# Two Fourier and gated layers on one core: the matrix tests in one list, and a later or earlier place for four groups of work

## The chip, the core and the metric

The kernel runs on one core of a Trainium2 chip. The core has a matrix engine (TensorE, PE in the profile, with its weight loads as PEld), VectorE (DVE), ScalarE (ACT), GpSimd (POOL), and SyncE (SP), which here issues the DMAs. Each engine runs its own instructions in order, and waits for the others at semaphores. The metric is the device time of one execution in microseconds; a kernel's time is the median of several runs.

## The reference

x has 2048 rows of 640. Two layers follow each other, each of a Fourier part A and a gated part B, both behind a layer norm and added to x:

```
def _A_ref(x, dft_seq_re, dft_seq_im, dft_hid_re, dft_hid_im):
    a = jnp.einsum("bsd,ed->bse", x, dft_hid_re)
    b = jnp.einsum("bsd,ed->bse", x, dft_hid_im)
    return jnp.einsum("ts,bse->bte", dft_seq_re, a) - jnp.einsum("ts,bse->bte", dft_seq_im, b)

def _B_ref(x, w_gate, w_up, w_down):
    g = jnp.einsum("bsd,df->bsf", x, w_gate)
    u = jnp.einsum("bsd,df->bsf", x, w_up)
    return jnp.einsum("bsf,fd->bsd", _sigmoid(g) * u, w_down)

x = x + _A_ref(_layernorm(x, axis=-1), ...)
x = x + _B_ref(_layernorm(x, axis=-1), ...)
x = x + _A_ref(_layernorm(x, axis=-1), ...)
x = x + _B_ref(_layernorm(x, axis=-1), ...)
```

w_gate and w_up are 640 x 1728, w_down (W2) is 1728 x 640. The Fourier matrices are 2048 x 2048 (sequence) and 640 x 640 (hidden, W_hid here), each with a real and an imaginary part. All are inputs.

## The kernel before, in words

The kernel has a fast version, `folded`, that holds if the Fourier matrices have the symmetries of such matrices and the weights lie in a range, and a slow one, `general`. The fast version runs always, tests its inputs on the way, and writes a flag; the slow one runs behind it if the flag says so, which it does not here. The 100 matrix tests are these: 64 row tests of the sequence matrices (`load_rows`, `test_rows`: 32 for each part, four DMAs of 128 KB each; five VectorE operations, then a square with a sum on ScalarE, `square_rest`), 20 column tests (`load_cols`, `test_cols`), and 10 row tests and 6 column tests of W_hid (`load_hidden_rows`, two DMAs of 160 KB, and `load_hidden_cols`). A test loads into one of three slots (`within(n % 3, ...)`): two stand beside the big memory, the third, "room", is taken from it. In the kernel before, layer 1 tests the real part of the sequence matrix (42 tests), and layer 2 the imaginary part and then W_hid (58 tests, W_hid's last).

Products are made of pairs of float16 parts, a high and a low one, so every operand is split: ScalarE writes the high part, VectorE the rest (`split`, L240 and L242).

A layer goes so. First comes the Fourier part ("he" to "b0" in the marks; layer 1's is in the hand-ordered opening). Then the gated part in two passes over halves of the rows, h = 0 and 1. A pass makes gate and up for tiles of 128 of the 1728 columns: in `seven(j)` and `four(j)` for most (a scheme with fewer products, in which sums of weights and of inputs are multiplied; L1108), in `gate_up` for the first tiles of the first pass (L1064). The results go from PSUM by copies on ScalarE (`snap`, L1112) and additions on VectorE (L1158, L1173); the sigmoid (L1115) and the multiplication `up` (L1188) follow some steps later, by `due(n, ...)`, which counts steps. Then a "down" multiplies by W2: layer 1's first with plain products (`down`, L1250), the other three with the seven combinations of W2's quarters (`stage`, L1364, with `rest_products`, L1345), each of which ends in a VectorE addition to x (`rows_add`, L1238).

The seven combinations of W2 are made once, in layer 1's second pass: `load_forms` (L1274 to L1277, three DMAs of W2 from HBM), `make_forms` (four GpSimd subtractions and a maximum on VectorE, L233), `split_forms` and `keep_forms` (stored to HBM as kept_f); `load_stage(s)` (L1312) loads one combination for a down. In the same way `load_s` (L1037 to L1043) loads the gate weights G, the sums S and the weights U of a tile, planned 15 us ahead of it.

The rows of the second pass are prepared during the first down: `pair_apply` (the norm on ScalarE, L442), `pair_combine` (GpSimd, L492 to L495), `pair_parts` (L507 on ScalarE, L508 on VectorE) and `pair_transpose` (a transposing DMA from the buffer "pb" into XW, L524), for four pairs of row tiles i. Before that, the Fourier results of row groups ("quads") q = 1, 2, 3 are added to x (`combine`, `join_hidden`, `add_hidden`), and statistics made (`pair_stats`, `quad_scale`).

The order is written out by plan: `steps` is the list of TensorE's work, each with a duration written into the code (0.2158 us for a product of 512 columns, for example), T their running sum. `when(t, f, ...)` puts a job before the step that is running at plan time t; jobs of one step are put out in the order of t, and each engine receives its own instructions in that order. start_of(layer, ...) is the plan time of a mark: "c" for `gate_up` steps, "j" for tiles, "d" for a down, "t" for the last narrow tile, "e" for the end of the layer; c0, s0, s1, d0, d1 are short names for such times. The tests are spread over weighted spans of the plan: at_test(n) is the time of the n-th, test n is loaded at at_test(n), tested at at_test(n + 2), squared at at_test(n + 2.6).

All buffers lie in one memory of 390 units of 512 bytes per partition. `take(n, key)` takes the next place from the written list PLACES, and `drop` gives it back; a place that is taken again too early in time is safe, but the writer waits for its last reader.

## Time and profile before

| | us |
|---|---|
| median of 3 runs | 1173.96 |
| lowest, highest | 1173.51, 1175.69 |
| the profiled execution, its own time | 1174.1 |
| its span, first to last instruction | 1172.3 |
| PE, PEld, DVE, ACT, POOL busy | 1101.6, 622.1, 839.7, 577.3, 206.9 |

Stretches of the trace that the text names, from its start: opening 0 to 110; layer 1's `gate_up` 110 to 168, first pass to 256, first down to 350, second pass to 531, second down to 611; layer 2's Fourier part to 655, `gate_up` to 734, first pass to 823, first down to 916, second pass to 1086, second down to the end. In the profile's rows, L12 is line 12 of the kernel before; a group shows "out<-in" by the program's names, its count, its busy time and the mean duration of one in ns, and, behind the bar, the engine's idle time just before such instructions and what ended it. In a view in order of time the first two numbers are start and length, and a number in brackets is the idle time before, with what ended it. SPq is SP's queue of DMA issues.

### The profile page before, as it was taken

What the parts mean: (1) busy time and instruction counts of PE and PEld (TensorE: products, weight loads), DVE (VectorE), ACT (ScalarE), POOL (GpSimd) and SP (SyncE); (2) the same over time, 40 slices, a digit from 0 to 9 for tenths busy, and PEclk for the clock granted to TensorE, in tenths of its full rate; (3) what the DMA queues carried; (4) which work ended last, traced back from release to release, by engine and by line L of the source; (5) the groups of instructions that cost most, each with busy time, mean ns of one, the idle gap of its engine ahead of it and who ended that gap; (6) DMA issues with size and microseconds to landing.
All of it is one profiled execution on the core that took longest, in us unless ns stands there. A gap on an engine that the chain in (4) does not pass through costs nothing.

```text
span 1172.3 us, 17676 instructions
## 1 busy us (share of the span) xinstructions
PE 1101.6 (94%) x6330; PEld 622.1 (53%) x6330; DVE 839.7 (72%) x1642; ACT 577.3 (49%) x1117; POOL 206.9 (18%) x295
## 2 busy tenths in 40 slices
PE   5699999999989898989999999999996999997997
PEld 2467444456764333436777744444674544443675
DVE  7997789758457898788786659966956466632862
ACT  6865547755325555555214544764534345432430
POOL 2210141515322141113020100020412000000211
PEclk9999999999999899999999999999998999999999
DMA  9421874344886777886512038666556765324621
GB/s 267 143 89 58 199 224 169 122 134 162 201 215 233 240 223 254 258 270 194 149 66 80 2 71 185 214 202 191 166 117 153 238 222 172 109 97 133 204 76 71
DMA packets 181912, 192.59 MB, mean 164 GB/s; under 512 B 76314, under 2 KB 145331, under 8 KB 181814
## 3 DMA queue, kind: packets, MB, share of 16 engines
q1 hardware_dynamic: 181174, 188.75, 53.9%
q0 software_dynamic: 640, 2.62, 0.6%
q8 instruction: 51, 0.84, 0.3%
q14 instruction: 47, 0.39, 0.1%
HBM read 143.17 MB, written 31.90 MB: 149 GB/s over the span
## 4 chain that ended last, share of the span: by engine, by line
PE 67%; DMA 15%; DVE 11%; ACT 3%; issue 2%; SPq 1%; POOL 1%; DVEq 0%; ACTq 0%
PE acc L1108 26%; PE acc L1364 14%; PE acc L1064 11%; PE acc L1250 6%; PE acc L858 4%; DMA big<-in_wh 4%; DMA big<-in_ct 3%; PE acc L1345 2%; DMA big<-big 2%; PE acc L776 2%; DVE big L242 1%; PE acc L1217 1%; DMA big<-kept_U 1%; DVE big L1325 1%; DMA big<-kept_f 1%
## 5 line engine op out<-in xcount | busy, mean ns | idle before, releaser
L1108 PE MATMUL acc<-big 128*128 128x512 f16 x2160 | 477.5, 383 | 25.1 <-ACT big L1112 15.6
L1108 PEld LDWEIGHTS <-big 128*128 128x128 f16 x2160 | 212.8, 99 | 288.3 <-issue 33.0
L1364 PE MATMUL acc<-big 128*128 128x320 f16 x1512 | 216.5, 301 | 7.9 <-DVE big L1238 4.7
L1364 PEld LDWEIGHTS <-big 128*128 128x128 f16 x1512 | 148.9, 99 | 68.8 <-issue 7.6
L1112 ACT ACTIVATE big<-acc 128x512 f32<-128x512 f32 x160 | 93.5, 590 | 147.5 <-PE acc L1108 147.2
L1064 PE MATMUL acc<-big 128*128 128x512 f16 (+1 forms) x900 | 156.7, 336 | 0.0
L1415 ACT ACTIVATE big<-big 128x768 f32<-128x768 f32 (+8 forms) x106 | 79.3, 748 | 139.2 <-DVE big L1448 37.5
L1064 PEld LDWEIGHTS <-big 128*128 128x128 f16 x900 | 87.8, 98 | 67.9 <-issue 0.6
L1325 DVE TENSOR_TENSOR big<-big 128x512 f16<-128x512 f32 x126 | 93.9, 760 | 19.1 <-ACT big L1324 18.9
L1250 PE MATMUL acc<-big 128*128 128x320 f16 x656 | 89.6, 299 | 1.2 <-DVE big L242 0.8
L242 DVE SCALAR_TENSOR_TENSOR big<-big 128x640 f16<-128x640 f32 (+7 forms) x94 | 77.7, 850 | 12.6 <-ACT big L240 12.6
L1238 DVE SCALAR_TENSOR_TENSOR big<-acc,big 128x320 f32<-128x320 f32 x112 | 52.8, 484 | 45.5 <-PE acc L1345 24.2
L1324 ACT ACTIVATE big<-big 128x512 f16<-128x512 f32 x126 | 72.0, 616 | 14.8 <-DVE big L1325 7.9
L1250 PEld LDWEIGHTS <-big 128*128 128x128 f16 x656 | 64.2, 98 | 26.6 <-POOL big L1019 1.0
L240 ACT ACTIVATE big<-big 128x640 f16<-128x640 f32 (+8 forms) x94 | 63.5, 705 | 28.2 <-DMA big<-in_wd 11.3
L1339 POOL TENSOR_TENSOR big<-big 128x512 f32<-128x512 f32 x18 | 28.4, 1602 | 250.5 <-DVE big L1325 249.4
L507 ACT ACTIVATE big<-big 128x384 f16<-128x384 f32 (+2 forms) x56 | 36.6, 667 | 51.5 <-DVE big L492 12.4
L508 DVE TENSOR_TENSOR big<-big 128x384 f16<-128x384 f32 (+2 forms) x56 | 45.7, 825 | 20.2 <-ACT big L507 13.3
L1158 DVE TENSOR_TENSOR big<-big,acc 128x512 f32<-128x512 f32 x40 | 27.3, 682 | 41.9 <-PE acc L1108 36.0
L1115 ACT ACTIVATE big<-big 128x512 f32<-128x512 f32 x80 | 49.8, 623 | 13.0 <-DVE big L1158 7.0
L430 POOL TENSOR_SCALAR rowt<-rowt 128x1 f32<-128x1 f32 x24 | 14.6, 609 | 229.5 <-ACT big L429 227.8
L858 PE MATMUL acc<-big 128*128 128x321 f16 (+3 forms) x324 | 49.0, 300 | 2.6 <-DVE big L900 1.5
(193 smaller groups left out, 1264.0 us busy)
## 6 DMA issues: line engine op xcount, KB each, us to landing
big<-in_ct SPq DMA_DIRECT2D x256, 128.0 KB
big<-kept_f SPq DMA_DIRECT2D x63, 320.0 KB
big<-kept_S SPq DMA_DIRECT2D x33, 512.0 KB
big<-kept_w SPq DMA_DIRECT2D x33, 320.0 KB
big<-in_ct SPq DMA_DIRECT2D x32, 256.0 KB
big<-kept_G SPq DMA_DIRECT2D x21, 320.0 KB
kept_S<-big SPq DMA_DIRECT2D x13, 512.0 KB
big<-in_wg SPq DMA_DIRECT2D x19, 320.0 KB
```

Source lines behind the costliest of these rows:

```text
L240: nc.scalar.activation(dh, src, AF.Copy, scale=s)
L242: nc.vector.scalar_tensor_tensor(dl, src, s, dh, op0=OP.mult, op1=OP.subtract)
L858: nc.tensor.matmul(ps[:m, :EC], z[:, at : at + m], w[:, 384 * wp : 384 * wp + EC], start=(d == 0 and zp == HI and wp == HI), stop=(d == ND ...
L1064: nc.tensor.matmul(ps, w[wp][:, d * P : (d + 1) * P], xt[:, xp, :], start=(d == 0 and wp == HI and xp == HI), stop=(d == ND - 1 and wp == LO))
L1108: nc.tensor.matmul(ps, wt, xt, start=start and n == 0, stop=n == len(todo) - 1, skip_group_check=not start)
L1112: nc.scalar.activation(dst, ps, AF.Copy)
L1238: nc.vector.scalar_tensor_tensor(xe, ps[:, :EH], CB, xe, op0=OP.mult, op1=OP.add)
L1250: nc.tensor.matmul(held["pd", i, e][0][:, :EH], held["t", half, j].parts[hp][:, i * P : (i + 1) * P], held["w", 2, j].parts[wp][:, e * EH ...
L1324: nc.scalar.activation(h, v, AF.Copy)
L1325: nc.vector.tensor_tensor(l, v, h, op=OP.subtract)
L1364: nc.tensor.matmul(ps[:, :EH], a[n][hp][:, i * P : (i + 1) * P], w[n][:, wp], start=fresh and m == 0, stop=m == len(todo) - 1, skip_group_ ...
L1415: nc.scalar.activation(v, v, AF.Square, accum_out=new_sum()[:p])
```

## The change

Five things are changed; the steps of TensorE stay the same.

- The tests of both parts stand in one list over both layers, r = 0 first, with W_hid's 16 put in as every fourth test from the 30th on; the spans and their weights are new (layer 1's is weighted 0.5 from its first down to its end), so that 31 tests lie in layer 1 and 69 in layer 2. Slot 2 is taken once for all. The two edge tests stand behind tests 20 and 28. Squares are put at at_test(n + 2.85), not 2.6. In `test_rows`, two VectorE operations of 256 elements become one of 512.
- W2's combinations: the first is loaded 12 us before the second pass (it was 6 us behind its start), one each 21.5 us; make_forms stands 13 us behind its load (it was 5). In the downs, the weights of stage 1 are loaded at d + 0.5 (was d - 7) and of stage 2 at d + 5 (was d + 2).
- Sigmoids are due a step later (3, not 2), and `up` too (5, not 4).
- In layer 2, quads 2 and 3 and their statistics move to the times that layer 1 has, up to some 30 us later; the four pairs of the first down begin at d0 + 8, 22, 49, 62 (were 11, 26, 41, 56), in layer 1 at d0 + 2, 22, 54, 70 (were 2, 22, 42, 62).
- PLACES is a new list.

```diff
-            due(2, lambda: sigmoid(hv(0)))
+            due(3, lambda: sigmoid(hv(0)))
...
-            due(2, lambda: sigmoid(hv(1)))
-            due(4, up)
+            due(3, lambda: sigmoid(hv(1)))
+            due(5, up)
...
     def room():
-        if which[0] == 2:
-            return held["room"].f32
+        if which[0] >= 2:
+            return held["room", which[0]].f32
...
-        nc.vector.tensor_tensor(b, a, b, op=same)
-        nc.vector.tensor_tensor(d, c, d, op=same)
+        bd = v.rearrange("p (g two c) -> p g two c", g=2, two=2)
+        nc.vector.tensor_tensor(bd[:, :, 1], bd[:, :, 0], bd[:, :, 1], op=same)
...
-        for q, u, pace in ((1, q1, 1.2), (2, s0 + 2, 3) if first else (2, c0 + 22, 1.5), (3, s0 + 28, 3) if first else (3, s0 + 6, 2.5)):
+        for q, u, pace in ((1, q1, 1.2), (2, s0 + 2, 3), (3, s0 + 28, 3)):
...
-                when(s0 + ((24, 50) if first else (6, 26))[q] + 4 * i, pair_stats, 1, i, q, True)
-            when(s0 + (70 if first else 46) + q, quad_scale, 2 + q)
+                when(s0 + (24, 50)[q] + 4 * i, pair_stats, 1, i, q, True)
+            when(s0 + 70 + q, quad_scale, 2 + q)
         for i in range(TB):
-            u = d0 + 2 + 20 * i if first else d0 + 11 + 15 * i
+            u = d0 + ((2, 22, 54, 70) if first else (8, 22, 49, 62))[i]
...
-                u = s1 + 6 + 22 * n
+                u = s1 - 12 + 21.5 * n
                 when(u, load_forms, n)
-                when(u + 5, make_forms, n)
+                when(u + 13, make_forms, n)
                 for k in range(2):
-                    when(u + 9 + 5 * k, split_forms, n, k)
-                    when(u + 12 + 5 * k, keep_forms, n, k)
+                    when(u + 14 + 7 * k, split_forms, n, k)
+                    when(u + 18 + 7 * k, keep_forms, n, k)
...
-                when(d - (16, 7, -2)[s] if s < 3 else ds[s - 2] + 1, load_stage, s)
+                when(d - (16, -0.5, -5)[s] if s < 3 else ds[s - 2] + 1, load_stage, s)
...
+    tests = []
+    for r in range(2):
+        tests += [(load_rows, test_rows, (r, k)) for k in range(2 * NS)]
+        tests += [(load_cols, test_cols, (r, i, k)) for i in range(NB + 1) for k in range(2)]
+    more = [(load_hidden_rows, test_hidden_rows, (r, k)) for r in range(2) for k in range(5)]
+    more += [(load_hidden_cols, test_hidden_cols, (r, j)) for r in range(2) for j in range(3)]
+    for n, test in enumerate(more):
+        tests.insert(30 + 4 * n, test)
+    spans = [(start_of(0, "d", 0) + 6, start_of(0, "e"), 0.5),
+             (start_of(1, "c", 1, 0) + 5, start_of(1, "j", 0, JC), 0.7), (start_of(1, "j", 0, JC), start_of(1, "d", 0), 1.0),
+             (start_of(1, "d", 0), start_of(1, "j", 1, 0), 0.4),
+             (start_of(1, "j", 1, 0), start_of(1, "d", 1), 1.1), (start_of(1, "d", 1), start_of(1, "d", 1) + 30, 0.6)]
+    pace = sum((b - a) * w for a, b, w in spans) / len(tests)
...
+    when(at_test(2) - 0.2, take, CK, "room", 2)
+    for n, (load, test, key) in enumerate(tests):
+        when(at_test(n), within, n % 3, load, *key)
+        when(at_test(n + 2), within, n % 3, test, *key)
+        when(at_test(n + 2.85), square_rest)
```

## The prediction

> **What bounds the kernel now.** I read the page first, then the busy times of TensorE by stage, then who waited for whom in the stages that lose time, then single rows in order of time.

> ```profile
> span 1172.3 us, 17676 instructions
> PE 1101.6 (94%) x6330; PEld 622.1 (53%) x6330; DVE 839.7 (72%) x1642; ACT 577.3 (49%) x1117; POOL 206.9 (18%) x295
> ```

> TensorE bounds the kernel; its instructions and their order are the same in both kernels. So only its stops count: idle time, and the half-speed clock that follows some stops. In the rows by stage, the columns are the stretch, its length, then busy time and count of each engine, the granted clock, DMA share and GB/s.

> ```profile
> 110.10:168.40 58.30, 58.30 (x272) 26.46 (x271) 46.24 (x75) 32.72 (x54) 14.79 (x16) 1.00 0.73 195
> 256.50:350.50 94.00, 89.57 (x657) 64.08 (x656) 61.02 (x108) 38.50 (x71) 34.70 (x40) 1.00 0.72 188
> 350.50:530.60 180.10, 165.46 (x732) 72.94 (x733) 147.52 (x289) 98.36 (x179) 34.50 (x48) 0.96 0.78 245
> 530.60:610.60 80.00, 79.53 (x586) 57.17 (x585) 65.75 (x137) 27.85 (x53) 14.22 (x17) 1.00 0.42 124
> 733.90:822.70 88.80, 88.14 (x409) 39.89 (x408) 67.62 (x145) 57.03 (x120) 9.53 (x24) 1.00 0.62 202
> 822.70:916.20 93.50, 84.09 (x586) 58.52 (x585) 64.83 (x104) 38.24 (x67) 25.60 (x22) 0.95 0.60 153
> 916.20:1007.50 91.30, 91.30 (x426) 41.42 (x424) 57.02 (x120) 43.55 (x86) 4.21 (x4) 1.00 0.61 197
> 1007.50:1086.30 78.80, 69.39 (x311) 30.29 (x310) 29.80 (x53) 26.26 (x58) 0.00 (x0) 0.98 0.35 114
> ```

> Loss of a stage = length minus PE busy, plus (1 - clock) times the length. A, first down of layer 1 (second row): 4.4. B, second gate/up pass of layer 1 (third): 14.6 + 0.04 x 180.1 = 21.8. C, first pass of layer 2 (fifth): 0.7. D, first down of layer 2: 9.4 + 4.7 = 14.1. E, second pass of layer 2 (last two rows): 9.4 + 1.6 = 11.0. Together 52.0 us can be won. The opening keeps its order, and the first and fourth rows (first chunks and second down of layer 1) lose 0 and 0.5.

> ```profile
> PE acc L1108 <- ACT big L1112: 14.5, 7, 4.5
> DVE wmax L233 <- DMA big<-in_wd: 22.0, 5, 8.0
> ACT big L507 <- DMA big<-big: 12.1, 1, 12.1
> ACT big L442 <- DMA big<-big: 17.3, 1, 17.3
> DVE big L1503 <- DMA big<-in_wh: 40.7, 9, 6.7
> PE acc L1108 <- DMA big<-kept_G: 6.1, 2, 4.4
> ```

> These are waits (total, times, longest): the first two in B, the third in A, the fourth in D, the last two in E. In B, TensorE waits for ScalarE's copies out of PSUM, but ScalarE is only late because VectorE stands 22.0 us before the maximum in make_forms. In A and D, ScalarE stands before memory that a transposing DMA still reads. In E, VectorE stands for W_hid rows, and TensorE for G weights behind them in SP's queue.

> **The change part by part.** A plan time below is the kernel's own clock for an order (a step's time is a constant in the code); d is a down's start, s a pass's. Engines run in order, ahead of TensorE where they need nothing from it.

> *B: W2's combinations and the tests.*

> ```profile
> 384.52 0.38 SPq L1274 DMA_DIRECT2D big<-in_wd  x1
> 391.88 1.49 DVE L233 TENSOR_REDUCE wmax<-big 128x1 f32<-128x1280 f32 x1 [5.04 <-DMA big<-in_wd]
> 399.86 26.22 PE L1108 MATMUL acc<-big 128*128 128x512 f16 x108 [4.49 <-ACT big L1112]
> 403.70:457.10 53.40, 49.68 (x217) 21.65 (x216) 46.95 (x96) 28.83 (x53) 16.03 (x22) 0.95 0.79 235
> L1445 DVE TENSOR_TENSOR big<-big 128x256 f32<-128x256 f32 x24 | 10.7, 448 | 1.7 <-DMA big<-in_ct 1.7
> L1446 DVE TENSOR_TENSOR big<-big 128x256 f32<-128x256 f32 x24 | 9.9, 414 | 2.0 <-DMA big<-in_ct 1.9
> L1448 DVE TENSOR_TENSOR big<-big 128x128 f32<-128x128 f32 x48 | 11.9, 290 | 0.8
> L1336 DVE TENSOR_TENSOR big<-big 128x512 f32<-128x512 f32 x23 | 15.7, 682 | 0.0
> L1462 DVE TENSOR_REDUCE cmax<-big 128x1 f32<-128x256 f32 x5 | 2.1, 411 | 0.0
> L1465 DVE TENSOR_TENSOR big<-big 128x256 f32<-128x256 f32 x5 | 2.1, 425 | 0.2
> ```

> A load of W2 lands 391.88 - 384.52 = 7.4 us after its last issue; the plan gives it 5 us, the change 13. The five waits sum to 22.0 with a longest of 8.0, and 8 more us of lead cover each, if the queue is no later than now. B holds 24 row tests and 5 column tests; the new order leaves 16 row tests. A row test costs VectorE (10.7 + 9.9 + 11.9) / 24 = 1.35 us, a column test (four operations, first and last shown) 4 x 2.1 / 5 = 1.7. Gone: 8 x 1.35 + 5 x 1.7 = 19.3. One 512-element operation for two of 256 saves 0.448 + 0.414 - 0.682 = 0.18 a row test, 2.9 over 16. So 147.5 - 22.2 = 125 us of VectorE work stand against 180.1 - 21.8 = 158 of TensorE's: on the whole there is room. In the middle third there is less: 46.95 busy, minus four of its nine tests (5.4) and 0.9 for five merged is 40.7, against 53.4 minus its loss (3.7 + 2.7) = 47.0; with the small waits of each tile that is nearly full. I leave 5 us of B's 21.8: **-17** (bounds -20, all but 2; and -8, when the leads are eaten up by a later queue). Only one set of W2's loads, three DMAs, falls into A, where SP takes 0.4 us for one.

> *Sigmoids and squares later.*

> ```profile
> L1115 ACT ACTIVATE big<-big 128x512 f32<-128x512 f32 x80 | 49.8, 623 | 13.0 <-DVE big L1158 7.0
> L1415 ACT ACTIVATE big<-big 128x768 f32<-128x768 f32 (+8 forms) x106 | 79.3, 748 | 139.2 <-DVE big L1448 37.5
> ```

> ScalarE stands 13.0 us before sigmoids and 139.2 before squares, and its PSUM copies queue behind them. A step or a quarter of a test more between producer and reader takes these waits off; the multiplication after a sigmoid moves with it by one step (1.3 to 1.9 us), and is read by a conversion planned 9 us after the tile. The gain is in B's and E's terms; by itself 0. The other side of the squares is a rival below.

> *D: quads 2 and 3 and the place table.*

> ```profile
> 864.05 5.17 SPq L524 DMA_TRANSPOSE big<-big  x1
> 871.95 6.22 SPq L524 DMA_TRANSPOSE big<-big  x1
> 880.14 0.92 ACT L442 ACTIVATE big<-big,rowt 128x640 f32<-128x640 f32 x1 [17.27 <-DMA big<-big]
> 895.76 3.82 PE L1364 MATMUL acc<-big 128*128 128x320 f16 x18 [3.98 <-DVE big L1238]
> 902.61 6.22 SPq L524 DMA_TRANSPOSE big<-big  x1
> 916.18 4.05 PE L1108 MATMUL acc<-big 128*128 128x512 f16 x18
> ```

> Pair 2's rows are written over pair 1's transposed source: planned at d+41, freed only at 880.14, d+57, 2.0 us after its issue ended at 878.17. The new table puts them over pair 0's, planned at d+49, and pair 0's transpose (864.05 + 5.17 + 2.0 = 871.2, d+48.5, and pair 1 before it is 4 us earlier) has landed then. Its second buffer goes over pair 1's, at d+53, with pair 1's transpose now right behind pair 0's: 4 + 2.6 (one test's four issues less) earlier than 880.1, d+51. So the 14.1 us go. What is late next: the last pair's parts move from d+66 to d+72. Now its transpose ends at 908.83, lands by 910.8 and leaves 5.4 us to 916.18; six later, and behind three issues of a weight load (0.4 each), it lacks 1.8. Stage 1's weights are loaded 7.5 us later, at d+0.5, and needed at d+9.8, and a W_hid test of 6 us is queued ahead: 1.5 (0 to 3). Stage 6's stand behind two transposes and another such test: 1.5 (0 to 3). D: -14.1 + 4.8 = **-9** (bounds -14 and -4).

> *A.* The table takes away the 12.1 us wait of the same kind; the last pair comes 8 us later. The 3.2 us that TensorE waits for its transpose at the end become 0 to 8: **-1** (bounds -4, +4). In layer 1's first chunks the table does the opposite: pair 1's source is laid over pair 0's while that is being transposed. ScalarE stands up to 8 us there (6.22 + 2.0), with 32.7 of 58.3 us busy, and the transposes are needed at the end of that row: 0. The second down of layer 1 takes three tests more (4 us), with VectorE 65.75 of 80.0 busy: 0.

> *C and E: more tests, W_hid's spread out.*

> ```profile
> 1053.75 12.29 SPq L1499 DMA_DIRECT2D big<-in_wh  x4
> 1049.56 3.14 SPq L1037 DMA_DIRECT2D big<-kept_G  x1
> 1060.76 9.63 PE L1108 MATMUL acc<-big 128*128 128x512 f16 x36 [4.44 <-DMA big<-kept_G]
> 1026.50:1036.00 9.50, 9.50 (x46) 4.32 (x45) 2.98 (x5) 2.87 (x6) 0.00 (x0) 1.00 0.14 52
> ```

> A W_hid row test takes two DMAs of 3.1 us, during which the engines move 52 GB/s at a share of 0.14. Ten follow each other now, and G, planned 15 us ahead, comes late. In the new list three others stand between two of them, 18 us or more apart, so the queue recovers each time: 6.2 us of delay against 15 of lead. E's cause goes; in exchange E holds 35 tests for 28 (counted in the two orders), one each 4.5 us, and a slot of three comes round in 13.5. I leave 4 of 11.0: **-7** (bounds -10, 0). C holds 17 tests for 15, four of them W_hid's; VectorE has 67.6 of 88.8 busy and two row tests are 2.7 us: **+2** (bounds 0, and +8 if each W_hid test delays a copy by 2).

> Sum: -1 - 17 + 2 - 9 - 7 = -32. Against the profiled execution's own 1174.1 us (span 1172.3 and 1.8 around it), which stands 0.1 above the median of 1173.96: **1142 us**.

> ```profile
> 433.30:440.30 7.00, 4.97 (x17) 1.89 (x16) 6.93 (x16) 6.01 (x13) 0.00 (x0) 0.76 0.89 290
> ```

> The rest that I leave (52.0 - 32 = 20) is idle and clock together; here a stop of 2.0 us is followed by a clock of half speed (0.76 over 7 us). [...]

> **The rivals.** *All is covered*: every lead suffices, 5 us are left of 52: 1174.1 - 47 = 1127. For it: the new table reuses memory much later; against it: VectorE's middle third. Chance 0.12. *The waits move*: W2's loads wait in a queue that is as late as now (B -8), D's last pair and weights pay their upper bounds (D -4), E -4, C +2, A 0: 1160. For it: the leads are counted in TensorE's time, and SP issues in order. This holds the case that the change doesn't do what it says. Chance 0.25. *Slower*: a test slot is loaded again 0.15 of a test (0.7 us) after its square is put into ScalarE's order (0.4 of a test before), so SP stands at each test, and the G loads behind it come late in the 20 tiles of layer 2. At 3.0 us a tile (mean of the two waits for G in E, 6.1 / 2) that is 60; with A, B and D as above and E's 11.0 replaced, 1174.1 - 27 - 11 + 60 = 1196. It decides from 38 / 20 = 1.9 us a tile; its point is the order of squares and slot loads. Against it: SP waits for squares in E today and G is late only behind W_hid. Chance 0.10.

> **How the numbers follow.** My forecast has 0.53, its own range 1132 to 1152. The range 1127 to 1166 leaves out the slower case and the outer ends of the two others, together 0.18. A difference within 0.2% (2.3 us) cannot be told from none; 0.02 for that, 0.88 faster, 0.10 slower.

> **What would show it.** B: VectorE's wait for in_wd below 5 us, and the stage near 163. D: no ScalarE wait above 5 us for a transpose, the stage near 84, and a stop of about 2 us at its end. E: no wait for kept_G above 2. Wrong, if W_hid's loads still hold G back, or if VectorE is busy without a break in B's middle third and TensorE loses as much there as now.

## The result and the profile after

The changed kernel takes 1134.86 us (median of 4 runs, 1133.52 to 1135.14), the kernel before 1173.74 beside it: a ratio of 0.9663, 95% interval 0.9646 to 0.968. The forecast was 1142 with a range of 1127 to 1166. The profiled execution took 1134.67 us.

The page of the changed kernel begins so:

```profile
span 1132.9 us, 17628 instructions
PE 1092.0 (96%) x6330; PEld 621.2 (55%) x6330; DVE 835.6 (74%) x1578; ACT 575.4 (51%) x1117; POOL 215.7 (19%) x295
```

TensorE's work is the same, so the 39.4 us of span came out of its stops and its slow clock (the granted clock is 0.994 over the span, for 0.986 before). The busy times by stage, in the columns of the prediction, are A, B, C, D, and E in two parts:

```profile
256.46:349.56 93.10, 89.43 (x657) 64.11 (x656) 56.05 (x87) 37.02 (x63) 40.72 (x44) 0.99 0.75 199
349.56:510.37 160.81, 160.81 (x733) 72.28 (x734) 132.45 (x229) 86.00 (x157) 34.11 (x44) 0.98 0.70 215
713.62:801.68 88.06, 88.06 (x409) 39.95 (x408) 67.20 (x129) 55.57 (x120) 8.33 (x24) 1.00 0.53 171
801.68:885.03 83.35, 79.65 (x585) 57.14 (x584) 66.60 (x107) 39.95 (x73) 26.67 (x22) 1.00 0.73 191
885.03:970.00 84.97, 82.63 (x376) 37.06 (x376) 47.35 (x93) 39.97 (x83) 4.70 (x4) 0.98 0.66 215
970.00:1046.86 76.86, 76.86 (x357) 34.85 (x356) 53.50 (x104) 39.06 (x82) 0.00 (x0) 1.00 0.58 189
```

Stage by stage, with the terms of the forecast:

| stage | before | after | moved by | forecast |
|---|---|---|---|---|
| A, first down, layer 1 | 94.0 | 93.1 | -0.9 | -1 |
| B, second pass, layer 1 | 180.1 | 160.8 | -19.3 | -17 |
| C, first pass, layer 2 | 88.9 | 88.1 | -0.8 | +2 |
| D, first down, layer 2 | 93.4 | 83.3 | -10.1 | -9 |
| E, second pass, layer 2 | 170.1 | 161.8 | -8.3 | -7 |

B has no stop of TensorE left. From A's beginning on, three stops of more than 2 us are left. In order of time, TensorE's rows with a number in brackets (the stop, and what ended it):

```profile
349.56 1.86 PE L1108 MATMUL acc<-big 128*128 128x512 f16 x4 [3.20 <-DVE quad L415]
885.03 2.29 PE L1108 MATMUL acc<-big 128*128 128x512 f16 x5 [3.19 <-DMA big<-big]
926.43 1.89 PE L1108 MATMUL acc<-big 128*128 128x512 f16 x8 [2.34 <-ACT big L1112]
```

The first two stand at the ends of A and D, where the second pass needs the last pair's transposed rows. (The first one's releaser is put down to VectorE; in the repeated run below the same stop is ended by the transposing DMA.) The third is in E. What VectorE and ScalarE did just before it:

```profile
924.75 0.49 DVE L1503 TENSOR_TENSOR big<-big 128x320 f32<-128x320 f32 x1 [7.01 <-DMA big<-in_wh]
925.33 0.47 ACT L1415 ACTIVATE big<-big 128x320 f32<-128x320 f32 x1 [5.14 <-DVE big L1503]
925.80 1.06 ACT L1112 ACTIVATE big<-acc 128x512 f32<-128x512 f32 x2
```

A row test of W_hid still holds TensorE once: VectorE waits 7.0 us for the load, ScalarE 5.1 for the square behind the test, and the PSUM copy behind the square is late.

### The profile page after: what moved, and what is told of

The parts are those of the page before. It is cut to its first block, busy times and chain, and to the rows that moved or that the text cites. A ratio compares the mean times of both kernels' runs of the same rounds, so it can differ in the third digit from the quotient of the medians.

```text
span 1132.9 us, 17628 instructions
## 1 busy us (share of the span) xinstructions
PE 1092.0 (96%) x6330; PEld 621.2 (55%) x6330; DVE 835.6 (74%) x1578; ACT 575.4 (51%) x1117; POOL 215.7 (19%) x295
## 4 chain that ended last, share of the span: by engine, by line
PE 82%; DVE 9%; DMA 4%; ACT 2%; issue 2%; POOL 1%; SPq 1%; DVEq 0%; ACTq 0%
PE acc L1108 38%; PE acc L1064 14%; PE acc L1364 14%; PE acc L1250 6%; PE acc L858 4%; PE acc L1217 2%; PE acc L1345 2%; PE acc L776 2%; DVE big L242 2%; DMA big<-in_ct 1%; DMA big<-in_wh 1%; DVE big L1325 1%; DMA big<-big 1%; DVE big L1238 1%; DVE quad L415 1%
## 5 line engine op out<-in xcount | busy, mean ns | idle before, releaser
L1108 PE MATMUL acc<-big 128*128 128x512 f16 x2160 | 472.0, 381 | 9.0 <-DVE quad L415 3.2
L1108 PEld LDWEIGHTS <-big 128*128 128x128 f16 x2160 | 212.3, 98 | 267.4 <-issue 15.4
L1364 PE MATMUL acc<-big 128*128 128x320 f16 x1512 | 213.4, 299 | 1.0 <-DVE big L1238 1.0
L1112 ACT ACTIVATE big<-acc 128x512 f32<-128x512 f32 x160 | 93.8, 592 | 186.7 <-PE acc L1108 184.9
L1364 PEld LDWEIGHTS <-big 128*128 128x128 f16 x1512 | 147.9, 98 | 59.3 <-issue 1.4
L1415 ACT ACTIVATE big<-big 128x768 f32<-128x768 f32 (+6 forms) x106 | 79.0, 745 | 75.4 <-DVE big L1448 30.0
L1238 DVE SCALAR_TENSOR_TENSOR big<-acc,big 128x320 f32<-128x320 f32 x112 | 53.3, 486 | 55.1 <-PE acc L1345 29.6
L1250 PE MATMUL acc<-big 128*128 128x320 f16 x656 | 89.4, 299 | 0.5 <-DVE big L242 0.5
L1158 DVE TENSOR_TENSOR big<-big,acc 128x512 f32<-128x512 f32 x40 | 27.3, 683 | 45.9 <-PE acc L1108 27.0
L507 ACT ACTIVATE big<-big 128x384 f16<-128x384 f32 (+2 forms) x56 | 36.3, 668 | 48.4 <-DVE big L492 14.7
L1446 DVE TENSOR_TENSOR big<-big 128x512 f32<-128x512 f32 x64 | 47.1, 736 | 15.5 <-DMA big<-in_ct 15.5
L430 POOL TENSOR_SCALAR rowt<-rowt 128x1 f32<-128x1 f32 x24 | 10.0, 417 | 244.8 <-ACT big L429 243.1
L1115 ACT ACTIVATE big<-big 128x512 f32<-128x512 f32 x80 | 49.7, 621 | 9.0 <-DVE big L1158 6.6
```

The costliest lines, as they stand in the source:

```text
L1108: nc.tensor.matmul(ps, wt, xt, start=start and n == 0, stop=n == len(todo) - 1, skip_group_check=not start)
L1112: nc.scalar.activation(dst, ps, AF.Copy)
L1115: nc.scalar.activation(v, v, AF.Sigmoid, scale=SG)
L1238: nc.vector.scalar_tensor_tensor(xe, ps[:, :EH], CB, xe, op0=OP.mult, op1=OP.add)
L1250: nc.tensor.matmul(held["pd", i, e][0][:, :EH], held["t", half, j].parts[hp][:, i * P : (i + 1) * P], held["w", 2, j].parts[wp][:, e * EH ...
L1364: nc.tensor.matmul(ps[:, :EH], a[n][hp][:, i * P : (i + 1) * P], w[n][:, wp], start=fresh and m == 0, stop=m == len(todo) - 1, skip_group_ ...
```

## The experiments

All ratios are to the kernel before, measured in the same comparison. Its median was 1171.73 us beside the four runs from forms_alone to tests_alone, 1170.87 beside lead_5_again, hidden_last and the two runs of the squares, and 1172.13 beside the other four, so times of different comparisons are compared by their ratios. The stages are those of the profiled executions:

| run | median us | ratio (95%) | A | B | D | E |
|---|---|---|---|---|---|---|
| before | 1173.74 | 1 | 94.0 | 180.1 | 93.4 | 170.1 |
| forms_alone | 1168.33 | 0.9964 (0.9946 to 0.9982) | 93.9 | 175.1 | 93.4 | 169.5 |
| places_alone | 1160.18 | 0.9883 (0.9844 to 0.9921) | 93.5 | 181.8 | 80.6 | 169.6 |
| hidden_four_dmas | 1159.37 | 0.9876 (0.9838 to 0.9913) | 94.4 | 179.4 | 93.2 | 158.0 |
| tests_alone | 1149.82 | 0.9789 (0.975 to 0.9828) | 94.2 | 165.2 | 93.5 | 162.3 |
| the change | 1134.86 | 0.9663 (0.9646 to 0.968) | 93.1 | 160.8 | 83.3 | 161.8 |
| after_again | 1131.74 | 0.9656 (0.9631 to 0.968) | 92.4 | 159.7 | 82.8 | 162.0 |
| lead_5_again | 1132.01 | 0.9667 (0.9637 to 0.9697) | 91.0 | 158.9 | 83.7 | 161.8 |
| forms_undone | 1136.1 | 0.9705 (0.9678 to 0.9731) | 90.1 | 165.0 | 83.7 | 160.2 |
| sigmoids_undone | 1130.87 | 0.965 (0.9624 to 0.9676) | 92.6 | 161.1 | 82.0 | 160.7 |
| hidden_last | 1157.71 | 0.989 (0.9864 to 0.9916) | 92.2 | 158.0 | 82.6 | 175.8 |
| squares_at_2_98 | 1139.99 | 0.9741 (0.9705 to 0.9776) | 94.3 | 161.1 | 83.9 | 163.1 |
| squares_at_2_6 | 1135.27 | 0.9698 (0.9672 to 0.9724) | 92.4 | 159.7 | 83.7 | 160.7 |
| four_dmas_old_pairs | 1126.86 | 0.9611 (0.9587 to 0.9634) | 92.3 | 159.7 | 81.4 | 158.0 |

after_again is the changed kernel itself, measured beside forms_undone, sigmoids_undone and four_dmas_old_pairs:

> The changed kernel once more, on the chip of the next three runs, so that they are compared with it there: ratio to the kernel before 0.966 as in the first comparison (0.9646 to 0.968); the stages within 1 us of 93.1, 160.8, 83.3 and 161.8, but for the first down of layer 1, which the runs so far show between 91 and 94.

It came out as expected but for B, which is 1.1 us shorter, and shows how far a stage moves by itself: about 1 us in B, 0.7 in A and 0.5 in D.

### One part alone, in the kernel before

**forms_alone.** The times of W2's combinations:

```diff
-                u = s1 + 6 + 22 * n
+                u = s1 - 12 + 21.5 * n
                 when(u, load_forms, n)
-                when(u + 5, make_forms, n)
+                when(u + 13, make_forms, n)
-                    when(u + 9 + 5 * k, split_forms, n, k)
-                    when(u + 12 + 5 * k, keep_forms, n, k)
+                    when(u + 14 + 7 * k, split_forms, n, k)
+                    when(u + 18 + 7 * k, keep_forms, n, k)
```

> The kernel before, with only the new times of W2's combinations (load 12 us before the pass and then every 21.5 us, make_forms 13 us behind it, parts and stores likewise); the tests stay, places are changed only where the new times forbid the old ones. Theory (the lead is what counts): VectorE's five waits for in_wd (22.0 us) go, and the second pass of layer 1 falls from 180.1 to 166-172 us, since 29 tests still fill its VectorE; total 1160-1166 us. Rival (VectorE is full there, and a wait that goes is filled with tests): the waits go but the stage loses less than 4 us, total 1170 or more.

The waits of forms_alone, and its stage B:

```profile
DVE wmax L233 <- DMA big<-in_wd: 8.8, 1, 8.8
PE acc L1108 <- ACT big L1112: 10.4, 11, 1.8
```
```profile
350.29:525.36 175.07, 163.34 (x733) 72.31 (x733) 153.79 (x295) 96.65 (x179) 40.37 (x48) 0.98 0.80 252
```

Of 22.0 us of waiting, 13.2 went; the stage lost 5.0, and the run 0.36%. VectorE's busy time rose from 147.5 to 153.8 in a shorter stage, and TensorE still stops eleven times for ScalarE's copies. This is close to the rival: with 29 tests, a wait that goes is filled with work that was waiting too.

**tests_alone.** The changed kernel's list of tests with squares at 2.85 and the joined subtraction; everything else as before (the diff is the change's second half, from "def room" to "square_rest").

> The kernel before with only the new list of tests (31 in layer 1, 69 in layer 2, W_hid's as every fourth, one slot taken once, the joined subtraction, squares at 2.85); W2's combinations, sigmoids, quads, pairs and their places as before. Theory: the second pass of layer 2 falls by 6-9 us (W_hid's spread out), the second pass of layer 1 by 4-9 (less VectorE work, but the waits for in_wd stay above 10 us), the first down of layer 2 stays within 2 of 93.4; total 1156-1165. Rival (69 tests are too many for layer 2): its first pass, first down and second pass together get no shorter, total 1166 or more.

Its waits of the maximum, and stages B, D and E:

```profile
DVE wmax L233 <- DMA big<-in_wd: 16.5, 6, 7.9
```
```profile
350.50:515.71 165.21, 159.91 (x733) 71.89 (x734) 129.14 (x226) 86.46 (x157) 36.39 (x48) 0.99 0.71 224
807.02:900.49 93.47, 83.10 (x586) 58.05 (x584) 64.18 (x103) 39.94 (x73) 26.54 (x22) 0.95 0.67 156
900.49:1062.83 162.34, 159.63 (x735) 71.97 (x732) 102.98 (x199) 79.04 (x165) 4.20 (x4) 0.99 0.65 212
```

B falls by 14.9 us with 16.5 of the 22.0 us of waits still there, more than was expected; E falls by 7.8, D stays. This part alone makes 22 of the 39 us, and the run lies 6 us below the expected range. (A row test has four VectorE operations in the kernel before, three with the joined subtraction.)

**places_alone.** The same order of everything; 64 of the 912 numbers in PLACES, all taken in the two first downs, so that pair 2 and pair 3 do not lie over a source that a transposing DMA reads.

> The kernel before, same order of all work, only other places: in the two first downs pair 2's buffers and pair 3's source no longer lie over a source that a transposing DMA has just read (64 of 912 places move, all in those two stretches). Theory: ScalarE's waits of 17.3 us (layer 2) and 12.1 us (layer 1) go, the first down of layer 2 falls from 93.4 to 83-86 us, the first down of layer 1 from 94.0 to 92-94; total 1162-1167. Rival (ScalarE would have stood there anyway, for the pairs' statistics or behind VectorE): gain below 3 us, total above 1171.

D, and ScalarE's norms of pair 2, which stood 17.27 us before:

```profile
823.85:904.42 80.57, 79.48 (x585) 57.13 (x584) 65.00 (x104) 38.45 (x67) 25.83 (x22) 1.00 0.73 181
```
```profile
866.65 0.91 ACT L442 ACTIVATE big<-big,rowt 128x640 f32<-128x640 f32 x1
868.04 0.91 ACT L442 ACTIVATE big<-big,rowt 128x640 f32<-128x640 f32 x1
```

No brackets: the wait is gone, and D falls by 12.8 us, more than by the whole change (10.1 and 10.6 in its two profiles). So the places make the gain, and the rest of the change costs D some 2 to 3 us. A moved by 0.5. Here too the run lies below its expected range (1162 to 1167), as hidden_four_dmas does (1164 to 1169).

**hidden_four_dmas.** The same bytes of W_hid in twice as many, smaller DMAs, with four column groups in the slowest dimension for two:

```diff
-            nc.sync.dma_start(v[:, g, :EH], bass.AP(wh.tensor, (r * D + row) * D, [[EH, 2], [d * D, 64], [1, EH]]))
+            for q in range(2):
+                nc.sync.dma_start(v[:, g, 160 * q : 160 * q + 160], bass.AP(wh.tensor, (r * D + row + 32 * d * q) * D, [[160, 4], [d * D, 32], [1, 160]]))
```

> The kernel before, only each W_hid row test's two DMAs of 160 KB become four of 80 KB with the slowest dimension 4, not 2 (the row's column groups of 160). Theory (these slow DMAs hold the queue, so G is late): they land faster, VectorE's waits for in_wh (40.7 us) fall below 15, no wait for kept_G stays, and the second pass of layer 2 falls from 170.1 to 161-165; total 1164-1169. Rival (ten such tests in a row are late because their slots come free late, not because of the DMA): the waits for in_wh stay above 25 us and the gain is below 2 us.

SP's issues of these loads (shortest, median and longest in ns), first in the kernel before, then in hidden_four_dmas, where the line is 1500:

```profile
L1499 SPq DMA_DIRECT2D big<-in_wh x20: 524/3168/4810, 1000.1 to 1070.5; - x20
```
```profile
L1500 SPq DMA_DIRECT2D big<-in_wh x40: 528/530/1602, 998.0 to 1050.5; - x40
```

And its stage E:

```profile
915.34:1073.33 157.99, 157.99 (x735) 71.65 (x732) 91.94 (x180) 72.85 (x150) 4.61 (x4) 1.00 0.58 185
```

E has no stop left and is 12.1 us shorter, with the tests in a row and in their old places; its list of waits has none for in_wh or kept_G. The way in which these twenty DMAs were cut was the whole of E's loss. Where such loads make nearly all the traffic, the DMA engines now move 90 GB/s at a share of 0.28, against 52 at 0.14 in the prediction's row of the kernel before (1026.5 to 1036):

```profile
1020.00:1024.00 4.00, 4.00 (x20) 1.84 (x19) 1.32 (x3) 1.95 (x5) 0.00 (x0) 1.00 0.28 90
```

By these shares about 4.5 of the 16 engines are busy where 2.2 were, with a load of G among them.

### One part undone, in the changed kernel

**lead_5_again.** Only the load of W2 moves back to 5 us ahead of make_forms.

```diff
-                when(u, load_forms, n)
+                when(u + 8, load_forms, n)
```

> The changed kernel, but each load of W2 stands 5 us ahead of make_forms again (8 us later; all else as changed). Theory: VectorE stands for in_wd again (15-22 us in sum), and the second pass of layer 1 rises from 160.8 to 165-172 us; total 1139-1146. Rival (with 16 tests there, VectorE has room enough to take the waits): the waits come back but the stage stays below 163, total 1133-1137.

```profile
DVE wmax L233 <- DMA big<-in_wd: 13.3, 3, 4.7
```
```profile
347.92:506.84 158.92, 158.45 (x733) 71.55 (x734) 132.55 (x232) 86.19 (x157) 37.65 (x48) 1.00 0.70 222
```

The waits come back (VectorE 13.3 us in three) and B stays at 158.9: TensorE stops for 0.5 us in all. The rival holds: the lead by itself is worth nothing in B once the tests are thinner. (A is 1.4 us shorter than in after_again; why is told below.)

**forms_undone.** All times of W2's combinations as before (the diff of forms_alone, the other way).

> The changed kernel with all times of W2's combinations as before (first load 6 us behind the pass's start, every 22 us, make_forms 5 us behind it, parts and stores likewise). Theory after the first runs (thinner tests free VectorE, the lead hardly counts): the second pass of layer 1 stays at 158-163 us, total within 2 us of the changed kernel on this chip, though VectorE waits 10 us or more for in_wd. Rival (my prediction's: the lead carries the gain): the stage rises to 166 or more, total 5 us or more above.

The stage is 165.0, between the two; the run is 4.4 us above after_again. TensorE stops four times for ScalarE's copies, 6.2 us in all. ScalarE's own waits shortly before these stops, in order of time:

```profile
420.63 0.66 ACT L624 ACTIVATE big<-big,coef,quad 128x321 f32<-128x321 f32 x1 [3.79 <-POOL coef L613]
456.48 1.00 ACT L240 ACTIVATE big<-big 128x960 f16<-128x960 f32 x1 [2.98 <-DMA kept_o<-big]
478.99 1.00 ACT L240 ACTIVATE big<-big 128x960 f16<-128x960 f32 x1 [4.55 <-DMA big<-in_wd]
487.90 1.27 ACT L240 ACTIVATE big<-big 128x1280 f16<-128x1280 f32 x1 [4.11 <-DMA kept_f<-big]
```

Only one of the four is a load of W2. One is GpSimd's (its subtractions and the Fourier coefficients of the next layer meet), two are places that a store still reads. So the new times are worth some 5 us of B in both directions, forms_alone and here; here it is by where they put this work, not by the lead. How the 5 us divide among these meetings was not taken apart; two of them depend on the place table too.

**sigmoids_undone.** Sigmoids due at 2 and `up` at 4.

```diff
-            due(3, lambda: sigmoid(hv(0)))
+            due(2, lambda: sigmoid(hv(0)))
...
-            due(5, up)
+            due(4, up)
```

> The changed kernel with sigmoids two steps and up four steps behind again. The tests alone left 5.3 us of stops in the second pass of layer 1, W2's combinations and the sigmoids together took them away. If the sigmoids did, this run's second pass of layer 1 has 163-166 us and the total is 2-6 us above the changed kernel. If they did nothing, the stage is within 1.5 us of 160.8 and the total within 2.

B 161.1 and the total 0.9 below after_again: the later sigmoids did nothing that can be measured.

**hidden_last.** W_hid's sixteen tests behind the others.

```diff
-        tests.insert(30 + 4 * n, test)
+        tests.append(test)
```

> The changed kernel, but W_hid's sixteen tests stand at the end of the list again, one behind the other; same number of tests at the same times. Theory (the run of slow DMAs makes G late): waits for in_wh above 25 us and for kept_G come back, the second pass of layer 2 rises from 161.8 by 4-9 us; total 1139-1144. Rival (it was not their order but the slots and squares): it stays within 2 us, total 1133-1137.

The waits of hidden_last, from its second pass of layer 2 on, and its last two stages:

```profile
DVE big L1503 <- DMA big<-in_wh: 50.9, 9, 8.3
ACT big L1415 <- DVE big L1503: 39.9, 7, 7.9
PEld L1364 <- DMA big<-kept_f: 5.6, 1, 5.6
```
```profile
880.71:1056.52 175.81, 163.87 (x732) 72.70 (x732) 92.22 (x182) 75.74 (x158) 4.20 (x4) 0.97 0.53 169
1056.52:1144.90 88.38, 81.70 (x585) 57.55 (x583) 54.08 (x104) 24.76 (x54) 14.14 (x12) 0.98 0.36 123
```

E rises by 14 us and the last down, which takes 79.5 to 79.7 us in every other run, by 9 (79.5 to 88.4): the run of slow DMAs now reaches the loads of the last down's weights. The direction is my theory's; the price, 14 us in E alone, is above the 4 to 9 expected. With the thinner list, putting W_hid's tests apart is worth more than half of the change.

**squares_at_2_98 and squares_at_2_6.** Only the time of the square.

```diff
-        when(at_test(n + 2.85), square_rest)
+        when(at_test(n + 2.98), square_rest)
```

> The changed kernel, squares 0.02 of a test before their slot is loaded again (it was 0.15). Theory of the slower rival (SP stands for the square at each slot, so G is late): 1.9 us or more for each of 20 tiles of layer 2, total 1170 or more. My theory (a later square finds its test done, and SP's wait is within the 15 us of lead): within 2 us of the changed kernel, 1133-1137.

> The changed kernel with squares at 2.6 again. Theory: by itself nearly nothing, since VectorE is no longer late: ScalarE's waits before squares rise from 75 us to above 110, TensorE's stops for ScalarE's copies grow by 0-4 us in all, total 1134-1139. Rival (the later square is what keeps the copies on time): ScalarE's copies are late in the second pass of layer 2, which rises by 5 us or more; total 1140 or more.

At 2.98 the ratio lies clear above after_again's (0.9705 to 0.9776 against 0.9631 to 0.968), about 0.9% or 10 us, by the two profiles 5.4 us, spread over A (+1.9), B (+1.4), D (+1.1) and E (+1.1). So a square just ahead of its slot's load does cost, but in all stages a little, and not 1.9 us or more for each tile: both expectations missed. What grew most are the two stops at the ends of A and D, which a transposing DMA ends (4.36 and 3.75 us, for 2.51 and 2.64 in after_again); TensorE and its weight loads wait 0.4 us for G in the whole run. At 2.6 ScalarE waits 99.4 us before squares (above 110 was expected), not 73.1 as in after_again, and the intervals of the two ratios overlap, so the time cannot be told from the changed kernel's.

### A version that beats both

**four_dmas_old_pairs.** The changed kernel with hidden_four_dmas' loads, layer 2's quads and pairs as before, layer 1's last pair at d0 + 66, and places to match:

```diff
-            u = d0 + ((2, 22, 54, 70) if first else (8, 22, 49, 62))[i]
+            u = d0 + ((2, 22, 54, 66) if first else (11, 26, 41, 56))[i]
```

> The changed kernel with W_hid's row tests in four DMAs of 80 KB, layer 2's quads and pairs at the times before the change (but no place over a source that a transposing DMA reads), and layer 1's last pair 4 us earlier. Theory from the runs alone: first down of layer 2 83.3 to 80.6, second pass of layer 2 161.8 to 158.0, first down of layer 1 to 90-92; total 6-9 us below the changed kernel on this chip. Rival (the gains need the old list of tests): less than 3 us below.

```profile
799.72:881.08 81.36, 79.65 (x585) 57.14 (x584) 65.75 (x106) 39.65 (x73) 26.72 (x22) 1.00 0.76 183
881.08:1039.07 157.99, 157.99 (x733) 71.61 (x732) 102.08 (x197) 79.19 (x165) 4.21 (x4) 1.00 0.65 213
```

1126.86 us (1124.94 to 1127.01) against 1131.74 (1130.51 to 1133.11) for the changed kernel beside it: 4.9 us, less than the 6 to 9 expected. E gives 4.0, D 1.4, A nothing: moving layer 1's last pair 4 us earlier left its stop at 2.4 us.

## Why the prediction was right, point by point

**The frame** held: TensorE's work is fixed, only its stops in A to E were to be won, and the sum came to -39.4 where -32 was forecast. Every term has its sign but C's, and the 7.4 us lie mostly in B (2.3), C (2.8), E (1.3) and D (1.1).

**A: right in its sum, with one price missed.** ScalarE's wait of 12.1 us is gone with the places alone, which gave 0.5, no more than A moves by itself. The prediction took the three loads of W2 that fall into A at 0.4 us of SP each. In after_again they stand right ahead of the last pair's transpose, and in forms_undone behind it; its issue, first in after_again, then in forms_undone:

```profile
338.10 8.09 SPq L524 DMA_TRANSPOSE big<-big  x1
```
```profile
337.08 6.53 SPq L524 DMA_TRANSPOSE big<-big  x1
```

It ends 2.6 us earlier, and TensorE's stop at the end of A, 2.51 us in after_again, is gone (1.16 in lead_5_again, where the loads also come behind it). By A's length the early load costs 1.4 to 2.3 us; moving the last pair 4 us earlier did not help where these loads still stand ahead of it (four_dmas_old_pairs).

**B: the size was near, the reason half wrong.** "TensorE waits for ScalarE's copies out of PSUM, but ScalarE is only late because VectorE stands 22.0 us before the maximum" is the step that failed. In the changed kernel the waits are gone, as forecast:

```profile
372.68 1.48 DVE L233 TENSOR_REDUCE wmax<-big 128x1 f32<-128x1280 f32 x1
```

But with most of them left and thinner tests B gains 14.9 (tests_alone), with most of them gone and the old tests 5.0 (forms_alone), and with 13.3 us of them brought back nothing is lost (lead_5_again). What paid most was the thinner list of tests: where it leaves room to catch up, a wait for a load is harmless. That VectorE's room did it is argued, not shown, since the same list also takes work from ScalarE (98.4 to 86.5 us busy in B) and from the DMA engines (a share of 0.78 to 0.71). That -17 came within 2.3 us of what was measured is in part luck, since the waits, which it took for the cause, gave 5.0 by themselves. And the middle third, which I put at 40.7 of 47.0 us, is this in the changed kernel:

```profile
403.20:456.80 53.60, 53.60 (x250) 24.27 (x248) 53.00 (x90) 32.58 (x57) 16.75 (x22) 1.00 0.72 223
```

VectorE is busy 53.0 of 53.6 us there and TensorE does not stop. VectorE's busy share did not decide it here, and the 5 us that I left for it were not needed.

**Sigmoids and squares, "by itself 0"**: shown for the sigmoids, and for the squares between 2.6 and 2.85.

**D: right, by its parts too.** ScalarE's wait is gone with the places alone (-12.8; forecast -14.1). The rest of the change costs D 2.7 (83.3 against 80.6; forecast 4.8), and nearly all of it is the stop for the last pair, which places_alone does not have; with layer 2's old quads and pairs (four_dmas_old_pairs) this stop is 1.2 us. It is 3.2, not 1.8: the last pair's transpose is issued from 874.98 on and takes 7.89, not 6.22 us,

```profile
874.98 7.89 SPq L524 DMA_TRANSPOSE big<-big  x1
```

and stages 1 and 6 do not wait for weights at all (forecast 3.0).

**E: right, with the price put at the wrong place.** W_hid's DMAs are the cause (hidden_four_dmas), and standing apart takes most of it away. But "6.2 us of delay against 15 of lead" took the price that these loads have in a row for the price of each. In a row, SP's issue of one takes 3.17 us in the median. Spread, the same issues in the changed kernel take 0.53 us:

```profile
L1499 SPq DMA_DIRECT2D big<-in_wh x20: 507/530/717, 559.7 to 912.1; - x20
```

The loads themselves stay slow. SP issues the last pair of them until 912.8, and VectorE's test, which waits for them, begins at 924.75. What is held is the issue right behind a pair, here one of a sequence load, whose median is 0.60 us:

```profile
912.89 4.29 SPq L1439 DMA_DIRECT2D big<-in_ct  x1
```

So the delay was not 6.2 us for each test, and it adds up only in a run; hence also the high price of hidden_last. "No wait for kept_G above 2" held; the one stop of 2.3 us left in E is W_hid's own.

**C: the +2 did not come.** It stood for two more row tests, 2.7 us of VectorE work. VectorE is busy 67.2 us there, for 67.6 before, and TensorE does not stop.

**The slower rival** had a point: with the square nearer to its slot's load the kernel is slower, but by 5 to 10 us as a whole where 60 were put, and at 2.85 it does not show. Its way, late loads of G, was not seen (0.4 us); whether SP's waits for squares are what makes the transposes late was not tested.

**The clock** was left in the rest of 20 us, together with idle time, and the changed kernel still loses by it: behind its stops of 3.2 us at the ends of A and D stand two stretches at 0.50, of 6.8 and 3.4 us, which is 5.1 us of lost clock.

## What to carry to other kernels

A wait that ends last in the trace is not always what pays: give the waiting engine slack, or take the wait away, and try both, since only one of them may move the end (here 14.9 us of B for the slack, 5.0 for the waits). Where an issue of a DMA is long in the trace, look at whether it is long alone too (here 3.17 us in a row and 0.53 apart), and at the share of the DMA engines meanwhile; where that is low (0.14 here), cutting the same bytes so that more engines work (0.28) can be worth more than moving the loads apart (158.0 against 162 us in E). When buffers are placed by a table, a place whose last reader is a slow DMA is a wait that no order of work shows (17.27 us here); moving 64 of 912 places was worth 1.2%.

## What was not expected of the hardware

What goes with it can be read from the same traces. Within one profile, all slow stretches behind the opening begin a whole multiple of 3.413 us apart: in the kernel before the first begins at 350.85, and those at 398.63, 436.18, 883.33, 896.98, 1060.82 and 1170.05 lie 14, 25, 156, 160, 208 and 240 times 3.413 us behind it. So each profile is cut here into pieces of that length, counted from its slow stretches, and the idle time of TensorE in a piece is set beside the clock of the next one. A stop of sigmoids_undone, then the piece that holds it and the next one (in the columns by stage, the idle time is the length minus PE's busy time, and the clock is the third number from the end):

```profile
348.61 2.97 PE L1108 MATMUL acc<-big 128*128 128x512 f16 x8 [2.19 <-DMA big<-big]
```
```profile
345.85:349.26 3.41, 1.22 (x9) 0.52 (x7) 3.41 (x7) 0.00 (x0) 0.04 (x1) 1.00 1.21 310
349.26:352.67 3.41, 3.41 (x10) 1.21 (x9) 0.85 (x3) 1.49 (x2) 0.00 (x0) 0.50 0.71 235
```

and a stop of squares_at_2_98, the two pieces that share it, and the next one:

```profile
887.26 2.10 PE L1108 MATMUL acc<-big 128*128 128x512 f16 x9 [3.75 <-DMA big<-big]
```
```profile
881.84:885.25 3.41, 1.67 (x13) 1.08 (x11) 1.58 (x4) 0.00 (x0) 0.00 (x0) 1.00 0.91 192
885.25:888.67 3.42, 1.41 (x7) 0.68 (x7) 0.00 (x0) 0.00 (x0) 0.00 (x0) 1.00 0.78 209
888.67:892.08 3.41, 3.41 (x18) 1.54 (x16) 0.02 (x1) 2.02 (x4) 0.00 (x0) 1.00 0.16 54
```

2.19 us in one piece have a slow one behind them; 3.75 us, split into 1.74 and 2.01, have none. In the changed kernel the stop of 2.34 us is split into 1.24 and 1.09 and has none either. Over the fourteen profiles, between the opening and TensorE's last product, of the pieces at full clock the 37 with a slow one behind them hold at least 1.99 us of idle time, and all others at most 2.01 (in the kernel before at least 2.03 and at most 1.88, in the changed kernel at least 2.12 and at most 1.38). A piece that is slow itself was followed by another slow one from 1.07 us of idle time on, and by none up to 0.66.

So by these profiles a stop of 2 to 3 us is to be priced at itself and, where 2.0 us of it fall into one piece, 1.7 us of lost clock, an estimate (half speed over 3.4 us). Where the pieces lie was not the same from one profile to the next: counted from the span's start the slow stretches begin 2.7 us behind a multiple of 3.413 in the kernel before, and 0.3 in the changed kernel. So beforehand this is a matter of chance. Why the clock falls, and whether it does so in other kernels, was not shown.
